# Attention and channel mixing on one core: the planner gives way to program order on all engines

## The chip, the core and the metric

The kernel runs on one core of one Trainium2 chip. The time is the device time of that core, in microseconds; two runs of the kernel before gave 1718.52 and 1720.22 us, a median of 1719.37. The profiled execution spans 1714.8 us. Everything is float32.

## What is computed

```python
scores = scale * q @ k.T                      # 8 batches, 8 heads, 576 x 64
thresh = max(scores, -1) - tau
scores = where(scores >= thresh, scores, -1e9)
attn   = softmax(scores) @ v                  # (+1e-9 in the denominator)
x      = heads side by side                   # (8, 576, 512)
u      = x + real(fft(fft(x, axis=1), axis=2))
un     = (u - mean(u)) / sqrt(var(u) + 1e-6)  # over the 512
out    = u + relu(un @ w_ch1) @ w_ch2         # 512 -> 2048 -> 512
```

The two heavy products at the end are done per group of 512 rows (nine groups), from the second group on with a two-level scheme of seven products of half-sized blocks (Strassen's kind), which saves products and costs additions of operands and results.

## The kernel before, in words

**Attention.** Heads go in pairs `n` (four pairs a batch, 32 in all). A pair has five steps `t`, so there are 160 steps `i = 5 n + t`, 20 to a batch; steps 0 to 3 hold 128 queries of both heads, step 4 the last 64 of both. One step is: `scores(i)` (TensorE, L427 or L433, into two large product banks `sc`); `softmax(i)`; and, one step later, `weights_in_parts(i - 1)`, which transposes the weights on TensorE (`pe` L530, `pw` L548) and copies them out on ScalarE (L536, L550; L540, L552 in step 4). At t = 3 and at t = 1 of the next pair `weighted_values` makes the products with v (L577).

**The softmax** is one function. For each of two heads: the negative maximum on VectorE (L451), the Exp on ScalarE (L459) and the threshold (L463), then on VectorE the masked product with its sum (L467) and the add of 1e-9 (L472); then the reciprocals (L481) and the scaling, one head on VectorE (L484), one on ScalarE (L488; step 4 copies 64 columns instead, L497). In the first eight pairs the scaling is done later, with a copy `rec` of the reciprocals on GpSimd (L493).

**Mixing.** After four pairs `fold_rows` folds their rows (VectorE for the last pair of a batch, GpSimd for the others), and `mixing(b)` makes the Fourier transforms: folds on VectorE (L661 to L670), products `py` (L680), then `pa` (L697, L701) with a copy on ScalarE (L713), two sums on VectorE (L717, L718) and sums into `u_t` on GpSimd (L720, L724).

**Products.** `two_level(g, rows)` is a generator. Its first stage has 28 blocks (L1045; results combined by ScalarE and by VectorE, L1014), its second 49 (L1195), seven for each of seven left operands. Between the blocks stand the sums that make operands: `l2_forms` for the next left operand (s1 to s4, L1121, shared by VectorE and GpSimd), `l1_form` (L1097), `s1_part` (L1026), and those that combine results: `gather` and `plus` (L1125), then `finish`, which adds to the rows (L789), and the stores. Jobs that are left at the end of a group lie in `pending` and are taken two at a time by `tick`, one tick for each first-stage block of the next group. For group 1 alone `w2_forms` (L897) remakes the second weights between the first-stage blocks, and `w1_forms` (L866) the first weights between the products of group 0.

**What sets the order.** `fill()` advances the mixing by one part and the products until they have spent their budget; it stands two or three times in each step and so spreads products between the pieces of attention. Up to step 39 the whole kernel stands in a manual schedule, in which each engine runs its instructions in the order in which the program names them. At L1501 `by_hand.close()` ends it, and L1502 opens one for TensorE alone: from step 40 TensorE keeps program order, and ScalarE, VectorE, GpSimd and the transfer queue are ordered by a planner, which works from the program's order and its own costs. All engines execute in the order that they are given. Product banks are a ring: four `mm` banks for everything but the scores.

## Time and profile before

Each row is a stretch of the profiled execution; busy times in us.

| stretch, us | what lies in it | TensorE | VectorE | ScalarE | GpSimd |
|---|---|---|---|---|---|
| 286.7 to 505.8 | steps 40 to 59, end of group 0, weights remade | 204.7 | 139.8 | 91.9 | 122.2 |
| 505.8 to 695.1 | steps 60 to 79 | 176.2 | 138.6 | 94.8 | 84.3 |
| 695.1 to 886.7 | steps 80 to 99 | 175.9 | 140.0 | 94.2 | 84.5 |
| 886.7 to 1077.1 | steps 100 to 119 | 174.1 | 137.5 | 94.5 | 84.0 |
| 1077.1 to 1270.6 | steps 120 to 139 | 176.2 | 140.7 | 94.2 | 84.4 |
| 1475.0 to 1714.8 | products without attention | 222.4 | 129.4 | 47.0 | 122.8 |

Over the whole span of 1714.8 us TensorE is busy 1574.0, VectorE 1199.5, ScalarE 795.0 and GpSimd 854.3. The mean granted TensorE clock is 0.966 of full speed.

How to read such views: a wait is idle time of an engine just before an instruction, with the instruction whose end released it. In a timeline each line has start, duration, engine, source line, operation, output and inputs, and in brackets the idle time before it. The names of tiles are the program's: `w_all` is the second weights' tile, reused as room for operands and results from group 1 on; `hs` the hidden values; `e` the softmax weights; `tmp` the two halves of the transform.

### The profile page before, as it was taken

To read this page: it belongs to the slowest core of one execution; us is meant where nothing else is said; L and a number is where in the kernel's file an instruction comes from. 1 tells how busy PE (TensorE), PEld (TensorE's weight loads), DVE (VectorE), ACT (ScalarE), POOL (GpSimd) and SP (SyncE) were. 2 spreads that over 40 slices of the span, in tenths; PEclk is the share of its full clock that TensorE was granted. 3 is DMA by queue.
4 is the path that set the end of the run, shared out by engine and by line. 5 is a ranking of instruction groups with operands and counts; after the bars stand their busy time and mean duration, and the time that the engine had idled before them with its cause. 6 is when DMAs were issued, how large, how long until landed. Compare 5 with 4: busy or idle time off the path is not lost.

```text
span 1714.8 us, 27077 instructions
## 1 busy us (share of the span) xinstructions
PE 1574.0 (92%) x9770; PEld 1215.3 (71%) x9770; DVE 1199.5 (70%) x2462; ACT 795.0 (46%) x1700; POOL 854.3 (50%) x961
## 2 busy tenths in 40 slices
PE   8998898998999899889989899889989899889997
PEld 4555454555788677777777678667778678879897
DVE  6987885566667767776677668786677768635646
ACT  5865664433535464445454454436444454222120
POOL 6784666267462434452363434452353434545536
PEclk9999999999999999999999999999989999999999
DMA  6433432545563435434453435424453423446755
GB/s 157 114 105 128 112 96 56 146 148 174 179 191 101 139 113 150 148 109 120 120 167 110 132 110 171 148 89 120 127 159 121 122 97 132 170 152 219 249 172 203
DMA packets 245499, 239.04 MB, mean 139 GB/s; under 512 B 196947, under 2 KB 214869, under 8 KB 225014
## 3 DMA queue, kind: packets, MB, share of 16 engines
q1 hardware_dynamic: 242854, 237.02, 45.0%
q8 instruction: 77, 1.26, 0.3%
q10 hardware_dynamic: 2512, 0.30, 0.1%
q14 instruction: 56, 0.46, 0.1%
HBM read 207.50 MB, written 29.62 MB: 138 GB/s over the span
## 4 chain that ended last, share of the span: by engine, by line
PE 55%; DVE 24%; POOL 10%; ACT 5%; issue 4%; DMA 2%; SPq 0%; DVEq 0%; ACTq 0%; POOLq 0%
PE ph L1045 20%; PE po L1195 10%; PE pv L577 6%; PE sc L427 6%; PE pw L548 4%; DVE e L467 4%; DVE w_all L1125 3%; DVE neg L451 3%; PE po L821 3%; DVE w_all L1121 2%; POOL w_all L1125 2%; PE ph L803 2%; ACT e L459 2%; POOL w_all L1121 1%; DMA w<-f 1%
## 5 line engine op out<-in xcount | busy, mean ns | idle before, releaser
L459 ACT ACTIVATE e<-sc,neg 128x576 f32<-128x576 f32 x288 | 211.7, 735 | 277.5 <-DVE neg L451 277.2
L451 DVE TENSOR_REDUCE neg<-sc 128x1 f32<-128x576 f32 x288 | 206.3, 746 | 117.5 <-PE sc L427 98.3
L467 DVE SCALAR_TENSOR_TENSOR e<-sc,thr,e 128x576 f32<-128x576 f32 x288 | 228.9, 814 | 57.2 <-ACT thr L463 56.2
L1195 PE MATMUL po<-w,w_all 128*128 128x128 f32 x1792 | 246.7, 292 | 9.4 <-ACT w_all L1207 4.9
L1195 PEld LDWEIGHTS po<-w,w_all 128*128 128x128 f32 x1792 | 231.1, 207 | 21.6 <-issue 9.9
L1121 POOL TENSOR_TENSOR w_all<-hs 128x512 f32<-128x512 f32 x72 | 97.8, 1359 | 227.4 <-PE po L1195 152.2
L1014 DVE TENSOR_TENSOR hs<-ph,hs 128x512 f32<-128x512 f32 (+1 forms) x128 | 105.2, 822 | 144.6 <-PE ph L1045 140.6
L548 PE MATMUL pw<-ident,e 128*128 128x128 f32 x1152 | 174.0, 278 | 20.5 <-ACT ends L536 5.3
L1045 PE MATMUL ph<-u_t,w 128*128 128x256 f32 x768 | 181.5, 382 | 4.3 <-ACT x L583 1.9
L427 PE MATMUL sc<-kT,qT 64*128 64x288 f32 x1024 | 176.1, 436 | 9.2 <-DVE e L467 9.1
L550 ACT COPY e_t<-pw 128x512 f32<-128x512 f32 x256 | 148.7, 593 | 49.2 <-PE pw L548 48.4
L548 PEld LDWEIGHTS pw<-ident,e 128*128 128x128 f32 x1152 | 137.4, 143 | 41.9 <-ACT ends L536 8.4
L1045 PEld LDWEIGHTS ph<-u_t,w 128*128 128x128 f32 x768 | 140.8, 190 | 30.8 <-issue 8.2
L1026 POOL TENSOR_TENSOR w<-hs 128x512 f32<-128x512 f32 x32 | 43.6, 1361 | 234.4 <-ACT hs L1022 222.6
L1045 PE MATMUL ph<-w_all,w 128*128 128x256 f32 x672 | 158.6, 383 | 1.5 <-DVE hs L1014 1.5
L427 PEld LDWEIGHTS sc<-kT,qT 64*128 64x128 f32 x1024 | 97.1, 189 | 66.8 <-issue 36.2
L1045 PEld LDWEIGHTS ph<-w_all,w 128*128 128x128 f32 x672 | 123.1, 190 | 23.6 <-issue 5.8
L1195 PE MATMUL po<-w,hs 128*128 128x128 f32 x960 | 127.2, 279 | 1.9 <-ACT ends L536 1.4
L488 ACT ACTIVATE e<-e,den 128x576 f32<-128x576 f32 x96 | 74.5, 776 | 106.4 <-DVE den L481 106.3
L1195 PEld LDWEIGHTS po<-w,hs 128*128 128x128 f32 x960 | 117.5, 194 | 7.9 <-issue 5.1
L1022 ACT ACTIVATE hs<-hs 128x512 f32<-128x512 f32 (+1 forms) x80 | 60.7, 759 | 78.5 <-DVE hs L1014 73.5
L484 DVE TENSOR_SCALAR e<-e,den 128x576 f32<-128x576 f32 x120 | 90.2, 751 | 3.5
(210 smaller groups left out, 2928.2 us busy)
## 6 DMA issues: line engine op xcount, KB each, us to landing
w<-f SPq DMA_DIRECT2D x152, 1024.0 KB, 4.9
hs<-in_moe_w_ch_dram SPq DMA_DIRECT2D x23, 512.0 KB, 4.7
q_in<-in_q_dram SPq DMA_DIRECT2D x128, 72.0 KB, 2.5
out_dram<-u SPq DMA_DIRECT2D x36, 256.0 KB, 2.3
k_in<-in_k_dram SPq DMA_DIRECT2D x124, 72.0 KB, 2.6
v_in<-in_v_dram SPq DMA_DIRECT2D x64, 128.0 KB, 2.4
f<-w SPq DMA_DIRECT2D x14, 512.0 KB, 4.3
f<-w SPq DMA_DIRECT2D x7, 1024.0 KB, 4.1
```

The lines of the kernel that those rows point to most:

```text
L427: nc.tensor.matmul(sc[j][:, c, 0:HALF], qT[hp, 128 * t : 128 * t + 128], kT[hp, k0 + HALF * c : k0 + HALF * (c + 1)], start=True, stop=True,)
L451: nc.vector.tensor_reduce(out=neg[:, j : j + 1], in_=sc[j][:, :, 0:HALF], axis=AXIS_XY, op=ALU.max, negate=True,)
L459: nc.scalar.activation(out=ej, in_=sc[j][:, :, 0:HALF], func=ACT.Exp, bias=neg[:, j : j + 1], scale=1.0)
L467: nc.vector.scalar_tensor_tensor(out=ej, in0=sc[j][:, :, 0:HALF], scalar=thr[:, j : j + 1], in1=ej, op0=ALU.is_ge, op1=ALU.mult, accum_out ...
L484: nc.vector.tensor_scalar(out=e[:, 0:S], in0=e[:, 0:S], scalar1=den[:, 0:1], scalar2=None, op0=ALU.mult)
L548: nc.tensor.transpose(pw[:, c, :], e[:, c0 : c0 + 128], ident[:, :])
L550: nc.scalar.copy(e_t[:, 4 * j : 4 * j + 4, qs], pw[:, :, :])
L577: nc.tensor.matmul(pv[64 * j : 64 * j + 64, 0:m], vt[:, 2 * c + j, :], e_t[:, 4 * j + c, 0:m] if c < 4 else ends[:, 0, 0:m], start=(c == 0 ...
L1014: nc.vector.tensor_tensor(out=to, in0=bank, in1=to if other is None else other, op=ALU.add)
L1045: nc.tensor.matmul(bank[:, 256 * q : 256 * q + 256].rearrange("p (two n) -> p two n", two=2), left[:, 256 * c + 128 * q : 256 * c + 128 * ...
L1121: eng.tensor_tensor(out=out_, in0=in0, in1=in1, op=op)
L1195: nc.tensor.matmul(to, lefts[m][j][:, s], right_[:, 128 * s : 128 * (s + 1)], start=jn in (0, 4) and s == 0, stop=s == 3, skip_group_check ...
```

## The change

It does five things, all of which act from step 40 on.

- `by_hand.close()` and the schedule for TensorE alone are taken out: all engines and the transfer queue keep program order to the end.
- The softmax becomes three functions, and the loop puts them between the stretches of products: maxima and Exp behind the scores and the values' products; masked products, one add for both denominators, reciprocals and the first scaling after the first `fill`; the second scaling after the transposes. The values' product is a generator too, so that its copy comes after the Exp.
- Sums that one engine made right after the other no longer change engines: in `l2_forms` s1 and s2 are VectorE's and s3 and s4 GpSimd's, in `l1_form` one operand is all VectorE's and one all GpSimd's.
- The gathers of three of the four results move to `pending`, and there to GpSimd (to VectorE in the last group only).
- The first pair's folding and row swap come later: `x_first` holds all 576 columns, and `fold_rows` copies it. The mixing of a batch starts at step 2 of the next batch and no longer at step 1.

```diff
+    def softmax_first(i):
...
+        for j in range(nh):
+            nc.vector.tensor_reduce(... negate=True)
+        for j in range(nh):
+            nc.scalar.activation(out=ej, in_=sc[j][:, :, 0:HALF], func=ACT.Exp, ...)
+            if j == 0:
+                nc.scalar.activation(out=thr[:, 0:nh], in_=neg[:, 0:nh], ...)
+    def softmax_second(i):
...
+        for j in range(nh):
+            nc.vector.scalar_tensor_tensor(... accum_out=den[:, j : j + 1])
+        nc.vector.tensor_scalar(out=den[:, 0:nh], ..., scalar1=1e-9, ...)
+        nc.vector.reciprocal(den[:, 0:nh], den[:, 0:nh])
+        nc.vector.tensor_scalar(out=e[:, 0:S], ..., scalar1=den[:, 0:1], ...)
+    def softmax_third(i):
...
+            nc.scalar.activation(out=e[:, S : 2 * S], ..., scale=den[:, 1:2])
...
-                (V if m == 1 else P, s1, x21, x22, ALU.add),
+                (V, s1, x21, x22, ALU.add),
                 (V, s2, s1, x11, ALU.subtract),
                 (P, s3, x11, x21, ALU.subtract),
-                (V, s4, x12, s2, ALU.subtract),
+                (P, s4, x12, s2, ALU.subtract),
...
-        at_slots(2, (4, 5, 6), l1_form(s1_tile, s1_tile, a11, (V, P, V, P))[0:3])
-        at_slots(3, (0,), l1_form(s1_tile, s1_tile, a11, (V, P, V, P))[3:4])
-        at_slots(4, (1, 2, 4, 6), l1_form(a12, a12, s1_tile, (V, P, V, P)))
+        at_slots(2, (4, 5, 6), l1_form(s1_tile, s1_tile, a11, (V, V, V, V))[0:3])
+        at_slots(3, (0,), l1_form(s1_tile, s1_tile, a11, (V, V, V, V))[3:4])
+        at_slots(4, (1, 2, 4, 6), l1_form(a12, a12, s1_tile, (P, P, P, P)))
...
-        at_slots(6, (2, 2, 3, 4, 4), gather(V, v_22))
-        at_slots(6, (5, 5), finish(1, 1, v_22))
...
-        pending.extend(gather(V, v_12))
-        pending.extend(gather(V, v_21))
+        last = g == NG - 1
+        for v in (v_22, v_21, v_12):
+            pending.extend(gather(V if last else P, v))
+        pending.extend(finish(1, 1, v_22))
+        pending.extend(finish(1, 0, v_21))
+        pending.append(stores(2, 3))
         pending.extend(finish(0, 1, v_12))
         pending.append(stores(0, 1))
-        pending.extend(finish(1, 0, v_21))
-        pending.append(stores(2, 3))
...
     late.append(True)
-    by_hand.close()
-    ctx.enter_context(tc.manual_schedule(engines={mybir.EngineType.PE}))
-    for i in range(2 * per_batch, total + 2):
+    for i in range(2 * per_batch, total + 3):
         if i < total:
             scores(i)
...
+        next(values, None)
+        if i < total:
+            softmax_first(i)
+        next(values, None)
+        if i % per_batch == 2:
+            while folds:
+                fold_more()
+            start_batch(i // per_batch - 1)
...
+        fill()
...
+        if i < total:
+            softmax_second(i)
+        weights = weights_in_parts(i - 1) if i <= total else iter(())
+        next(weights, None)
+        if t > 2 or i % per_batch == 1:
             fold_more()
         fill()
         next(weights, None)
         if i < total:
-            softmax(i)
+            softmax_third(i)
...
         fill()
```

## The prediction

> **What bounds the kernel now.** I read the sums by stretch first, then who TensorE waited for, then the timeline at the two waits that come back in every batch.
>
> The sums (us of the stretch, then busy time of each engine, then the granted TensorE clock). 286.7 us is where step 40 starts, the first step that the change touches; the four rows of 505.8 to 1270.6 are one batch of attention each.
>
> ```profile
> 286.70:505.80 219.10, 204.71 (x1072) 138.77 (x1071) 139.75 (x277) 91.93 (x198) 122.20 (x119) 0.96 0.52 159
> 886.70:1077.10 190.40, 174.14 (x1171) 142.16 (x1170) 137.48 (x292) 94.45 (x203) 83.97 (x98) 0.96 0.44 131
> 1270.60:1475.00 204.40, 184.15 (x1221) 151.09 (x1221) 142.21 (x295) 97.99 (x214) 87.35 (x98) 0.95 0.37 121
> ```
>
> TensorE is the bound and waits some 16 us in 190. Stretch less PE busy over all of 286.7 to 1714.8 is 114 us, of which some 10 is the drain after the last product: **104 us of idle TensorE** can be won. VectorE is busy 137 of 190, GpSimd 84. Who it waited for, after 286 us (us, times, longest):
>
> ```profile
> PE pe L530 <- ACT e L497: 23.8, 8, 4.8
> PE pa L697 <- DVE tmp L718: 21.8, 5, 4.7
> PE pn L763 <- ACT x L583: 6.2, 5, 1.3
> PE pe L533 <- POOL rec L493: 5.4, 1, 5.4
> PE ph L1045 <- POOL t_room L1001: 4.3, 1, 4.3
> PE po L1195 <- ACT ends L540: 4.3, 1, 4.3
> PE pw L548 <- DVE u L789: 3.8, 1, 3.8
> ```
>
> A dozen waits of about 4.5 us make up over half. The first kind, at the start of a batch, in order of time:
>
> ```profile
> 891.00 2.48 POOL L1121 TENSOR_TENSOR w_all<-w 128x512 f32<-128x512 f32 x2
> 892.29 1.73 DVE L1121 TENSOR_TENSOR w_all<-w_all,w 128x512 f32<-128x512 f32 x1 [6.69 <-POOL w_all L1121]
> 894.32 0.52 DVE L484 TENSOR_SCALAR e<-e,den 128x576 f32<-128x576 f32 x1
> 894.88 0.24 ACT L497 COPY e<-e 128x64 f32<-128x64 f32 x1 [9.26 <-DVE e L484]
> 895.17 0.47 PE L530 MATMUL pe<-ident,e 128*128 128x128 f32 x1 [4.81 <-ACT e L497]
> ```
>
> VectorE, in order, stood 6.69 us behind a GpSimd sum issued just before; the softmax it held back (L484) was all that the transpose needed. The second kind, five steps later: VectorE ran the gather sums L1125, L789 and the next step's maxima L451 before the two sums (L717, L718) that free a product bank:
>
> ```profile
> 946.62 1.14 DVE L1125 TENSOR_TENSOR w_all<-w_all 128x128 f32<-128x128 f32 x4
> 949.78 0.45 DVE L718 TENSOR_TENSOR tmp<-pa,tmp 128x289 f32<-128x289 f32 x1
> 950.37 0.40 PE L697 MATMUL pa<-seq_even,y_e 128*1 128x145 f32 x1 [4.67 <-DVE tmp L718]
> ```
>
> Each such wait costs twice. The stretch after the first:
>
> ```profile
> 894.30:901.10 6.80, 4.74 (x21) 4.34 (x22) 5.55 (x14) 5.69 (x14) 0.00 (x0) 0.50 0.01 2
> 960.00:970.00 10.00, 10.00 (x60) 7.85 (x57) 6.72 (x18) 4.67 (x9) 3.89 (x6) 1.00 0.68 231
> ```
>
> For 6.8 us after it the clock is 0.50: 21 products, where an undisturbed 10 us hold 60 (another product mix, with longer shapes). So a wait of 4.5 us costs 4.5 and then 6.8 x 0.5 = 3.4. The clock record has such windows after 286 us for 96 us in all, so **48 us of TensorE time** besides the 104.
>
> **What the Trainium skill says.** "TensorE: Matmul & The Clock Gate", Part 1, says that the array falls to half clock after an idle window of about 3.4 us that runs freely, and returns after a busy one. The trace agrees: waits of 3.5 us and more are followed by a window at 0.50, those of 1.3 us in steady stages are not. "SBUF — State Buffer", Who interferes with whom, says that a VectorE instruction with two SBUF inputs shuts out a GpSimd instruction that reads SBUF, and the reverse, one waiting for the whole of the other. The trace fits: the same 128x512 sum L1121 takes 0.81 us on average on VectorE in one form and 1.73 at 892.29, beside GpSimd. "GPSIMD Engine Reference", 4.1, puts two-input sums at about twice VectorE's time; here 1.36 us (GpSimd, w_all<-hs) against 0.81 to 1.13.
>
> **The change part by part.** The products, 5,635 instructions, are the same; only their order and that of the other engines moves.
>
> 1. *Program order on all engines from step 40.* Until now ACT, DVE, POOL and the queue were ordered by a planner from there. Step 39's reciprocal copy (rec L493) stood behind six GpSimd sums (L866, 2.35 us each); in order it comes first. That takes away 5.4 us, the 1.7 before it and (3.4 + 6.8) x 0.5 = 5.1 of half clock: **12 us**.
> 2. *No short-notice work.* In each left operand of the second stage VectorE makes s1 and s2, GpSimd s3 and s4, and s4 is used last of seven; a11's difference is all VectorE's. So no VectorE sum waits for a GpSimd one issued a product ago, bar the last quarter of a12. First kind: five waits of 4.49, 4.81, 4.52, 4.83 and 3.52 = 22.2, their windows (three of 6.8, one of 10.2, one of 3.4) x 0.5 = 17, and the copy wait of 1.2 after four of them = 5: **44 us**. The single 4.3 us (po <- ACT ends L540) is the same event at 516 us, with its window **8 us**.
> 3. *Gathers to GpSimd.* 105 VectorE sums leave (7 groups x 15): L1125's means of 0.44 (128x128) and 0.91 us (128x256), 3 and 2 of a gather, make 21 x (3 x 0.44 + 2 x 0.91) = 66 us less on VectorE; on GpSimd the rows of 0.83 and 1.04 give 21 x (2.5 + 2.1) = 96 us more, some 16 a batch on 84 of 190, hidden beside the first stage's products. With L717 and L718 straight after their products the second kind goes: 4.67 + 4.14 + 4.67 + 4.14 + 4.14 = 21.8, and 5 x 3.4 = 17: **39 us**.
> 4. *Softmax in three pieces.* 96 adds of 0.15 us go (two denominators in one), 14 us off VectorE. The maxima come behind the scores, the masked products one fill later, so that the Exp (0.74 each) runs beside other work; scaling is done a fill before the transposes need it. What a 9 us step has in slack is some 3 us. I book 0 for it alone.
> 5. *Moved.* The batch's mixing starts a step later (20b+2), with x_first held whole (one copy of 576 columns, about 1 us, for one of 0.44). Nothing waits for it but the last group: 0, bound +6 us at the tail. The transfer queue is in order too, so weight loads stand behind stores that wait for VectorE; but a load is issued two chunks ahead (7 us of products without attention) and lands in 4.9: 0.
> 6. *What program order loses.* The w2 forms of group 1 (L897) were spread by the planner from 314 to 425 us. In order they start at step 50 and go by one part per product block. Seven keeps, each a chain: GpSimd sum 1.44, VectorE, GpSimd sum 1.30, the DMA (4.1), while GpSimd also makes the form, 2 x 2.5: some 7.9 us, 55 in all, plus about 11 of GpSimd's other work (folds, u forms). VectorE stands in that chain with the softmax queued behind, and TensorE behind that. A block's 8 matmuls start 0.216 us apart, so 14 blocks are 24 us of products; attention takes some 3.9 of a 9.2 us step (scores 1.2, transposes 1.5, values and rest 1.2), which makes 42: loss 66 - 42 = 24, less a few us of slack: **+18 us**, bounds 0 (the chain fits) and 40 (with half clock). The 3.8 us wait of 403 us (u L789) and its window, 7, go; as they lie in the same disturbed stretch I count **-6**.
> 7. *New small waits.* The second sine copy now stands on ACT until four GpSimd sums (3.2 us) are done, a fill (about 3 us) after they start; ACT also waits for VectorE's maxima before it copies x. Nothing in the trace prices this: bounds 0 and 2 x 4.5 + 6.8 = 16 a batch, if both recurring waits came back. I take 3 a batch, **+15 us**.
>
> Sum: -12 - 44 - 8 - 39 + 18 - 6 + 15 = -76, so 1719 - 76 = **1643 us**.
>
> **The rivals.**
> - *Waits come back in other places* (0.20). For it: VectorE, busy 126 of 190 a batch after the change, waits in order for scores, Exp and banks, and forms stand in its way. Against: most steps have no idle TensorE even now. Forms at +40, and 6 us a batch with a half-clock window: 1719 - 103 + 40 + 30 - 6 = 1680.
> - *Nearly all goes* (0.12). In the last hand-ordered steps (240 to 286.7 us) TensorE was not idle at all. Forms fit in, no new waits, 10 us of the smaller waits gone too: 1719 - 103 - 6 - 10 = 1600.
> - *Slower: VectorE becomes the bound* (0.08). Its work of 126 a batch plus its present waits for scores, banks and Exp, some 40, is 166 of 191. If rigid order brings these to 70, a batch takes 196: 6 x 5 + 18 = +48, 1767. Against: the gathers gone are its most contended sums.
>
> **How the numbers follow.** Forecast 0.60. The border of 2% is 1685. Forecast, near-all and a third of the first rival lie below: 0.79 faster; the rest of the rival, 0.13, within; 0.08 slower. The range reaches from "nearly all" to past the first rival: 1600 to 1695.
>
> **What would show it.** Right: no row pe <- e (L547) or pa <- tmp (L788) of over 2 us; mean clock up from 0.966 to 0.98; VectorE's busy time down by some 80 us, GpSimd's up by 96; the batch from about 190 us to 174; steps 50 to 55 longer, with VectorE idle before the forms. Wrong: recurring waits of over 3.5 us elsewhere (ACT's tmp copy on GpSimd), or batches still at 190 with the two kinds gone, which would mean that VectorE sets the pace.

## The result, and the profile after

The changed kernel takes **1692.82 us** (1692.64 to 1692.99) against 1719.37 before: a ratio of 0.9846, 95% interval 0.9803 to 0.9888. It is faster by 26.5 us, or 1.5%: clear of the noise, but short of the 2% from which the forecast counted a time as faster (its border was 1685). The forecast was 76 us (1643); the time lies inside the stated range, near its upper end.

The same three rows of sums by stretch, of the kernel after: steps 40 to 59, one steady batch (steps 100 to 119), and the last batch with its mixing, which here is taken to 1450 (it holds 1,318 records of TensorE against 1,221 in the row of before, so their lengths are not to be compared). Columns as before: length, busy time of TensorE, weight loads, VectorE, ScalarE, GpSimd, granted clock, DMA share, GB/s.

```profile
285.80:528.10 242.30, 206.24 (x1012) 137.85 (x1011) 138.99 (x252) 91.12 (x193) 117.77 (x108) 0.91 0.52 161
...
892.60:1074.80 182.20, 173.21 (x1185) 142.30 (x1184) 132.19 (x261) 94.06 (x204) 93.69 (x113) 0.98 0.46 142
...
1255.30:1450.00 194.70, 187.18 (x1318) 154.69 (x1318) 140.82 (x273) 99.85 (x221) 99.95 (x120) 0.99 0.44 141
```

Two things are to be seen. The steady batch went from 190.4 to 182.2 at a clock of 0.98 instead of 0.96: that is the gain. Steps 40 to 59 went from 219.1 to **242.3** at 0.91 instead of 0.96: a loss, where the forecast had a sum of nothing (-12 + 18 - 6). By stretch, after less before: steps 40 to 59 +23.1, steps 60 to 139 -37.6, steps 140 to the last product -11.0, the drain +2.4, and -0.9 ahead of step 40.

Who TensorE waited for after 286 us (us in total, times, longest):

```profile
PE pw L598 <- ACT ends L586: 28.3, 9, 4.8
PE sc L427 <- DVE e L527: 9.7, 4, 7.0
PE ph L1115 <- DVE hs L1084: 7.3, 2, 7.0
PE ph L1115 <- DMA w<-f: 7.2, 2, 6.6
PE pw L598 <- ACT x L636: 6.5, 1, 6.5
PE py L750 <- DVE f L731: 5.0, 2, 4.6
PE ph L1115 <- POOL t_room L1071: 4.1, 1, 4.1
PE po L1263 <- DMA w<-f: 3.4, 1, 3.4
```

Both kinds of wait that the change was aimed at are gone: the list has no transpose `pe` behind the copy of `e` and no `pa` behind `tmp`. In their place stands a wait of the transposes `pw` behind the copy `ends`. It comes in each batch at step 17, 2.8 us, and at step 2, 3.7 to 4.8 us (in the first two batches 0.9 to 1.6, with some 2.3 more at step 3). The one of `py` on `f` is new too, and stands in the tail; that on `t_room` was there before. The longest of the other rows lie in steps 40 to 59, once each.

**Step 2.** VectorE's timeline up to the late maxima (first lines), then ScalarE and TensorE:

```profile
908.44 0.69 DVE L841 BATCH_NORM_STATS2 stats<-u 128x6 f32<-128x512 f32 x1 [2.51 <-ACT u L839]
...
913.64 0.81 DVE L680 TENSOR_TENSOR half<-x 128x287 f32<-128x287 f32 x2
914.38 0.95 DVE L685 TENSOR_TENSOR f<-half 128x143 f32<-128x143 f32 x4
...
915.32 1.26 DVE L694 TENSOR_TENSOR f<-x 128x2 f32<-128x2 f32 x1
...
917.10 1.48 DVE L859 SCALAR_TENSOR_TENSOR u<-w_all,rstd,u 128x256 f32<-128x256 f32 x1
...
918.50 1.41 DVE L506 TENSOR_REDUCE neg<-sc 128x1 f32<-128x576 f32 x2
919.33 1.28 ACT L512 ACT_TABLE_LOAD   x1 [5.75 <-DVE neg L506]
...
922.07 0.26 ACT L586 COPY ends<-pe 128x128 f32<-128x128 f32 x1
...
922.38 0.69 PE L598 MATMUL pw<-ident,e 128*128 128x128 f32 x4 [4.84 <-ACT ends L586]
```

VectorE stood 2.51 us for ScalarE, then folded the batch's last pair, and only then came the maxima (L506). ScalarE is in order too: it stood idle for 5.75 us in front of the Exp with the copies `ends` and `e_t` queued behind it. These copies free the product banks, and TensorE, out of banks, waited for them, although the rows that they copy had nothing to do with these maxima. Between maxima and Exp stands also an `ACT_TABLE_LOAD` of 1.28 us, which began only when the maxima were there (the load before it, at 908.43, is L849's). It is part of the 4.84 us, and none of the runs that go at this wait takes it away. At step 17 (1052.59) the same chain, without such a load, starts from three sums L1191 of 0.68, 1.64 and 1.76 us, the last two beside GpSimd's sums; a fourth, of 1.64, comes behind the maxima.

**Steps 40 to 59.** The longest wait, 318.60, with VectorE and GpSimd ahead of it:

```profile
302.96 2.97 DVE L680 TENSOR_TENSOR half<-x 128x287 f32<-128x287 f32 x2
305.85 5.81 DVE L685 TENSOR_TENSOR f<-half 128x143 f32<-128x143 f32 x4
...
306.46 4.78 POOL L936 TENSOR_TENSOR w<-w,w 128x1024 f32<-128x1024 f32 x2
...
311.81 1.41 DVE L506 TENSOR_REDUCE neg<-sc 128x1 f32<-128x576 f32 x2
...
314.90 2.81 DVE L710 TENSOR_TENSOR f<-f 128x608 f32<-128x608 f32 x1
...
318.60 2.51 PE L427 MATMUL sc<-kT,qT 64*128 64x288 f32 x7 [7.03 <-DVE e L527]
```

The four sums L685 took 5.81 us; the same four took 0.95 in the kernel before (as L615, at 309.87) and take 0.95 at 914.38 above. Beside them GpSimd remakes the first weights in sums of 2.4 us each. Behind the late maxima VectorE then made L709 and L710 (1.73 and 2.81 us; 0.77 and 0.79 at step 102) before the masked product L527 that frees the scores' bank. And the wait for weights at the start of group 1, with the transfer queue before it:

```profile
398.01 0.37 SPq L866 DMA_DIRECT2D out_dram<-u  x1
398.42 1.40 SPq L1020 DMA_DIRECT2D w<-f  x3
...
403.76 1.62 PE L1115 MATMUL ph<-u_t,w 128*128 128x256 f32 x3 [6.62 <-DMA w<-f]
```

The load was issued just behind a store of rows, which had waited for VectorE.

### The profile page after: what moved, and what is told of

Same layout as the page of the kernel before. It is cut to its first block, busy times and chain, and to the rows that moved or that the text cites. A ratio compares the mean times of both kernels' runs of the same rounds, so it can differ in the third digit from the quotient of the medians.

```text
span 1690.9 us, 27097 instructions
## 1 busy us (share of the span) xinstructions
PE 1562.0 (92%) x9770; PEld 1208.6 (71%) x9770; DVE 1176.6 (70%) x2253; ACT 793.4 (47%) x1700; POOL 918.7 (54%) x1074
## 3 DMA queue, kind: packets, MB, share of 16 engines
q8 instruction: 78, 1.28, 0.3%
## 4 chain that ended last, share of the span: by engine, by line
PE 68%; DVE 17%; ACT 5%; POOL 4%; issue 3%; DMA 2%; SPq 0%; DVEq 0%; ACTq 0%; POOLq 0%
PE ph L1115 21%; PE po L1263 16%; PE pv L629 8%; PE sc L427 7%; PE pw L598 5%; PE po L891 2%; PE ph L873 2%; DVE e L467 2%; DVE w_all L1191 2%; ACT e L512 1%; PE py L750 1%; DVE e L527 1%; PE sc L433 1%; DVE neg L506 1%; PE pa L767 1%
## 5 line engine op out<-in xcount | busy, mean ns | idle before, releaser
L512 ACT ACTIVATE e<-sc,neg 128x576 f32<-128x576 f32 x216 | 158.8, 735 | 239.0 <-DVE neg L506 238.6
L1263 PE MATMUL po<-w,w_all 128*128 128x128 f32 x1792 | 241.1, 287 | 7.4 <-DMA w<-f 3.4
L1263 PEld LDWEIGHTS po<-w,w_all 128*128 128x128 f32 x1792 | 224.9, 201 | 18.3 <-issue 6.5
L506 DVE TENSOR_REDUCE neg<-sc 128x1 f32<-128x576 f32 x216 | 154.0, 749 | 113.5 <-PE sc L427 102.8
L1115 PE MATMUL ph<-u_t,w 128*128 128x256 f32 x768 | 185.1, 388 | 14.7 <-DMA w<-f 7.2
L527 DVE SCALAR_TENSOR_TENSOR e<-sc,thr,e 128x576 f32<-128x576 f32 x216 | 168.2, 811 | 15.0 <-ACT thr L516 15.0
L1195 POOL TENSOR_TENSOR w_all<-w_all 128x128 f32<-128x128 f32 (+2 forms) x161 | 117.3, 744 | 23.1 <-DVE w_all L1280 10.2
L535 DVE TENSOR_SCALAR e<-e,den 128x576 f32<-128x576 f32 x120 | 84.7, 706 | 4.2
```

The source lines that it names most:

```text
L506: nc.vector.tensor_reduce(out=neg[:, j : j + 1], in_=sc[j][:, :, 0:HALF], axis=AXIS_XY, op=ALU.max, negate=True,)
L512: nc.scalar.activation(out=ej, in_=sc[j][:, :, 0:HALF], func=ACT.Exp, bias=neg[:, j : j + 1], scale=1.0)
L527: nc.vector.scalar_tensor_tensor(out=ej, in0=sc[j][:, :, 0:HALF], scalar=thr[:, j : j + 1], in1=ej, op0=ALU.is_ge, op1=ALU.mult, accum_out ...
L535: nc.vector.tensor_scalar(out=e[:, 0:S], in0=e[:, 0:S], scalar1=den[:, 0:1], scalar2=None, op0=ALU.mult)
L1115: nc.tensor.matmul(bank[:, 256 * q : 256 * q + 256].rearrange("p (two n) -> p two n", two=2), left[:, 256 * c + 128 * q : 256 * c + 128 * ...
L1195: return lambda: eng.tensor_tensor(out=to, in0=to, in1=other, op=ALU.add)
```

## The experiments

Each run has the kernel before on the same chip beside it; the ratio is to that. The last two columns are the lengths of two stretches in the run's trace (before: 219.2 and 764.7 us). 1% is 17 us. Traces of versions that are the same in steps 60 to 139 have 723.2 to 727.2 us there, and those that are the same in steps 40 to 57 have 240.6 to 244.4 in steps 40 to 59. A difference of under some 4 us between two traces therefore tells nothing by itself.

| kernel | us | ratio, 95% interval | steps 40-59 | steps 60-139 |
|---|---|---|---|---|
| changed kernel | 1692.8 | 0.9846 (0.9803-0.9888) | 242.3 | 727.2 |
| planner | 1730.5 | 1.0081 (1.0060-1.0101) | 217.6 | 771.9 |
| order_only | 1997.0 | 1.1615 (1.1566-1.1664) | 293.6 | 929.5 |
| one_piece | 1925.6 | 1.1217 (1.1182-1.1253) | 263.9 | 896.5 |
| hybrid60 | 1668.1 | 0.9722 (0.9707-0.9737) | 218.9 | 724.6 |
| w1_spread | 1684.3 | 0.9816 (0.9791-0.9841) | 238.8 | 723.2 |
| load_early | 1688.2 | 0.9827 (0.9811-0.9842) | 237.1 | 725.9 |
| w2_spread | 1687.2 | 0.9822 (0.9804-0.9839) | 238.9 | 724.5 |
| three_spread | 1676.5 | 0.9765 (0.9746-0.9784) | 225.8 | 725.7 |
| late_fold | 1690.2 | 0.9853 (0.9836-0.9871) | 243.9 | 721.1 |
| copies_first | 1689.1 | 0.9854 (0.9837-0.9871) | 244.4 | 719.3 |
| forms_only | 1681.2 | 0.9785 (0.9763-0.9807) | 244.4 | 712.4 |
| stats_only | 1685.2 | 0.9810 (0.9786-0.9834) | 240.6 | 721.9 |
| gather_v | 1698.1 | 0.9897 (0.9876-0.9919) | 244.2 | 724.7 |
| short_notice | 1699.5 | 0.9903 (0.9886-0.9920) | 241.5 | 728.5 |
| best1 | 1648.7 | 0.9613 (0.9593-0.9632) | 221.1 | 707.8 |
| all_in_order | 1652.7 | 0.9617 (0.9598-0.9635) | 220.6 | 707.6 |
| best2 | **1643.2** | 0.9564 (0.9548-0.9579) | 215.4 | 708.5 |

The theories: **A**, the loss against the forecast is a short list of waits that rigid order makes, each with a cause that can be taken away; **B**, VectorE is in effect the bound under rigid order, and a wait taken away comes back as another.

### Order and text apart

**planner**: the text of the changed kernel, with the two lines back that leave all but TensorE to the planner.

```diff
+    by_hand.close()
+    ctx.enter_context(tc.manual_schedule(engines={mybir.EngineType.PE}))
     for i in range(2 * per_batch, total + 3):
```

> The changed kernel with its new order of the program text, its new engine assignments and its three softmax pieces, but with ScalarE, VectorE, GpSimd and the transfer queue ordered by the planner from step 40 on, as in the kernel before. Theory A (the loss against the forecast is named waits, which rigid order makes): the 23 us that steps 40 to 59 lost come back in part, and the new waits at steps 2 and 17 of a batch go or change place; about 1675 us. Theory B (VectorE is in effect the bound, and one wait taken away comes back as another): within 10 us of the changed kernel's 1692.8. If it is over 1705, program order itself is the main gain of the change and the assignments are worth little.

1730.5 us, the figure of neither theory: the new text under the planner is slower than the old one. It keeps steps 40 to 59 as short as before, and takes 45 us more than the changed kernel in steps 60 to 139. Its timeline at the longest wait, which comes once in each of five batches (6.6 to 9.8 us):

```profile
964.98 2.62 POOL L1195 TENSOR_TENSOR w_all<-w_all 128x256 f32<-128x256 f32 x5
...
966.96 4.22 DVE L859 SCALAR_TENSOR_TENSOR u<-w_all,rstd,u 128x256 f32<-128x256 f32 x1 [7.41 <-POOL w_all L1195]
...
971.10 1.41 DVE L506 TENSOR_REDUCE neg<-sc 128x1 f32<-128x576 f32 x2
...
971.88 0.74 ACT L512 ACTIVATE e<-sc,neg 128x576 f32<-128x576 f32 x1 [14.09 <-DVE neg L506]
...
974.16 1.11 PE L598 MATMUL pw<-ident,e 128*128 128x128 f32 x4 [9.84 <-ACT ends L586]
```

The planner put VectorE's finishing sum (L859) ahead of the maxima, and it stood 7.41 us for a gather that is now GpSimd's. So the gathers on GpSimd want an order that puts their reader late. This is read from the trace; no run tried the planner with the gathers on VectorE.

**order_only**: the kernel before, with those two lines taken out and nothing else.

> The kernel before with one edit of the change alone: the schedule by hand is not closed at step 40, so that ScalarE, VectorE, GpSimd and the transfer queue keep program order to the end; softmax in one piece, gathers, short-notice sums and the mixing are those of before. The planner with the changed text gave 1730, program order from step 60 with it 1668. Theory P (program order is what gains, and the new text is a small help): 1690 to 1720 us. Theory Q (program order needs the softmax in pieces and the jobs placed for it; on the old text VectorE blocks at each step): over 1740 us, with waits of TensorE on e or ends at most steps.

1997 us, theory Q. **one_piece**: the changed kernel, with its three functions called one behind the other where the softmax stood before.

```diff
-        if i < total:
-            softmax_first(i)
...
-        if i < total:
-            softmax_second(i)
...
         if i < total:
+            softmax_first(i)
+            softmax_second(i)
             softmax_third(i)
```

> The changed kernel with its three softmax functions called one behind the other at the end of the step, where the softmax in one piece stood before, all else as changed (program order from step 40). Theory P (the pieces are what makes program order possible): over 1900 us, the waits of sc on e (L527) of over 100 us in sum as in the kernel before with program order alone. Theory R (the rest of the text does it): under 1750 us. The forecast had booked 0 for the pieces, that is 1693.

1925.6 us. The two greatest waits of TensorE after 286 us, of order_only first:

```profile
PE sc L427 <- DVE e L467: 191.5, 123, 13.5
```

and of one_piece:

```profile
PE sc L427 <- DVE e L527: 134.6, 75, 6.4
```

The next scores need the bank that the masked product reads. With the softmax at the end of a step this product comes after all that the fills have named, just before the scores, at nearly every step. The four corners are then:

| | planner from step 40 | program order |
|---|---|---|
| text before | 1719 | 1997 |
| text after | 1730 | 1693 |

Neither half of the change gains alone. And within the text it is the pieces that count most: without them 233 us of the 304 between 1997 and 1693 are lost again. What they would win alone, in the old text, was not run.

### Steps 40 to 59

**hybrid60**: the changed kernel, with the planner kept up to step 59 and program order from step 60.

```diff
+    by_hand.close()
+    planned = ctx.enter_context(ExitStack())
+    planned.enter_context(tc.manual_schedule(engines={mybir.EngineType.PE}))
     for i in range(2 * per_batch, total + 3):
+        if i == 3 * per_batch:
+            planned.close()
+            ctx.enter_context(tc.manual_schedule())
```

> The changed kernel with the planner kept for ScalarE, VectorE, GpSimd and the queue in steps 40 to 59 alone, and program order from step 60 to the end. Theory A: steps 40 to 59 took 242.3 us in program order and 219.2 in the kernel before; with the planner they go back to about 220, and the rest stays: about 1670 us. Theory B: what the stretch wins is not kept, since work is only put off: over 1685 us.

1668.1 us: steps 40 to 59 took 218.9, the rest is unchanged (724.6 to 727.2). 23 of the 50 us that the forecast missed are here, and they aren't given back later.

Which part of program order costs it? **w1_spread** names the parts of the first weights' forms (L936) less often:

```diff
+        slots = itertools.count()
...
-                    next(forms, None)
+                    if next(slots) % 3 == 2:
+                        next(forms, None)
```

> The changed kernel with the first weights' forms (L936, GpSimd sums of 2.4 us each) put one behind every third stretch of products of group 0 and no longer one behind each, the rest at its end. Theory A: VectorE's fold in step 42 no longer runs beside them (its four sums L685 go from 5.81 us back to about 1), the 7.0 us wait at step 43 and its window go: 10 us less in steps 42 and 43; part of it may be given back where the rest of the forms comes at the end of the group. About 1683 us. Theory B (GpSimd's amount of work, not its place): the wait moves, 1690 to 1700.

**load_early** issues the load of weights at the end of group 0 ahead of its last store:

```diff
+            if t == 2:
+                for _ in forms:
+                    pass
+                ensure(1)
             rows.add(t, slice(0, DM), po[:, :])
             rows.store(t)
...
-        for _ in forms:
-            pass
-        ensure(1)
```

> The changed kernel with the weight load at the end of group 0 issued before the last store of rows, so that it does not stand on the transfer queue behind a store that waits for VectorE. Theory A2 (the in-order queue): the 6.6 us wait at the first products of group 1 and its half-clock window (6.8 us at half) go, and steps 50 to 54 have 10 us less: about 1683 us. Theory A1 (the chain of keeps sets that stretch): what is won at its start is lost behind it, 1688 to 1693 us.

**w2_spread** names the parts of the second weights' forms (L967) half as often:

```diff
-                next(forms, None)
+                if at % 2 == part % 2:
+                    next(forms, None)
```

> The changed kernel, all in program order, with the parts of the second weights' forms (L967) put one behind every second first-stage block of group 1 and no longer one behind each: 28 blocks instead of 14 for the seven keeps. The planner kept for steps 40 to 59 gave back 25 us. Theory A1 (the chain of keeps is most of that, steps 50 to 54 being too short for it): the waits of 7.0 (hs L1084) and 6.5 us (x L636) and two of their three half-clock windows go, steps 50 to 59 lose some 15 to 20 us in sum, about 1675 us. Theory A2 (the in-order transfer queue is most of it): the 6.6 us wait for w stays and others come, under 8 us won, 1685 to 1693.

1684.3, 1688.2 and 1687.2 us: w1_spread as theory A had it, load_early as A1 and w2_spread as A2, which is to say that neither of these two alone is most of the loss. Each took its own wait away and won little. w1_spread: in place of the 7.0 us at step 43 stands a wait of 2.2. load_early: the 6.6 us went, and the waits of steps 52 to 54 grew from 17.3 to 21.3 us in sum. w2_spread: the 7.0 became 3.3 and the 6.5 went, and one of 7.1 us for weights came at 501 us, where a load (L1020) again stood on the queue behind a transfer of the forms. In steps 40 to 59 they won 3.5, 5.2 and 3.4 us of 242.3, about the spread of unchanged traces, and in time each lies inside the interval of the changed kernel, so that only the waits tell them from it. **three_spread** has all three.

> The changed kernel, all in program order, with the three edits of batch 2 together: first weights' forms one behind every third stretch of products, the weight load ahead of the last store of group 0, second weights' forms one behind every second block. Alone they gave 0.3, 0.2 and 0.25% of the time. Theory A (three causes that hide one another: each edit alone gives its wait to the next in the chain): together they give more than the sum of 12 us, steps 40 to 59 fall from 242 to about 222 as with the planner, about 1672 us. Theory A' (separate causes of their own sizes): the sum, about 1680 us. Theory B (VectorE is short of time in that stretch): under 6 us, 1687 or more.

1676.5 us, between the two figures expected. The stretch fell by 16.5 us, where the three alone sum to 12.1 and theory A had 20. With a spread of some 4 us a trace this leaves open whether they hide one another; that they are causes it shows. Two waits for weights are left, 7.2 and 3.1 us, both for loads on the in-order queue.

### Steps 2 and 17

**late_fold** names the second half of the last pair's fold one step later:

```diff
-        if i % per_batch == 1:
-            fold_more()
         fill()
```

> The changed kernel with the second half of the fold of a batch's last pair one step later, so that these VectorE sums come behind the maxima of step 2 and not ahead of them. Theory A (ScalarE waits for late maxima, and product banks wait behind its Exp): the wait of about 4.8 us of pw on ends at step 2 falls to about 1 and its half-clock window goes, the one at step 17 stays; some 6 us for each of five batches, about 1663 us to 1670. Theory B: the fold delays step 3 instead, and the time stays at 1690 to 1695.

**copies_first** puts the Exp and the masked products of steps 2 and 17 behind the copies that free the banks:

```diff
+    LATE_EXP = (2, 17)
...
-        if i < total:
+        if i < total and i % per_batch not in LATE_EXP:
             softmax_second(i)
...
         next(weights, None)
+        if i < total and i % per_batch in LATE_EXP:
+            softmax_exp(i)
+            softmax_second(i)
```

> The changed kernel with Exp and the masked products of steps 2 and 17 of each batch put behind the first part of the transposes and their copies, so that the copies that free product banks do not stand on ScalarE behind an Exp that waits for late maxima. Theory A: both recurring waits (4.8 and 2.8 us) fall under 1 us and their windows go: 7.6 + 3 or so for each of five batches, about 1640 to 1655 us. Theory B: VectorE gets its Exp later, the scaling is late, and the waits turn up at the next transposes: 1685 to 1700 us.

Neither gained in time; in their traces steps 60 to 139 won 6.1 and 7.9 us, a little over the spread. late_fold took 1.1 us off the wait at step 2 (4.8 to 3.7). copies_first did what it says: the waits of `pw` behind `ends` went. At step 17 a wait of 1.7 us took the place of 2.8. Its timeline one step after step 2:

```profile
1098.09 3.02 PE L427 MATMUL sc<-kT,qT 64*128 64x288 f32 x8 [3.48 <-DVE e L533]
```

With the Exp later, the masked product was later and the next scores waited for their bank. That is theory B for step 2: the maxima are late because VectorE is, and moving ScalarE's queue moves the wait. So the two runs that follow shorten what VectorE has ahead of the maxima.

**forms_only** moves sums at the start of the second stage:

```diff
-        for _ in l2_forms(1):
-            pass
+        first_forms = l2_forms(1)
+        next(first_forms)
+        next(first_forms)
...
+        at_slots(0, (0, 1), [lambda: next(first_forms)] * 2)
...
-            at_slots(at, (1, 2, 3, 5) if at == 3 else (0, 1, 3, 5), [next_form] * 4)
+            at_slots(at, (3, 4, 5, 6) if at == 0 else (1, 2, 3, 5) if at == 3 else (0, 1, 3, 5), ...)
```

> The changed kernel with one edit: at the start of the second stage s3 and s4 of the first left operand are named at slots 0 and 1, and the forms of the second operand at slots 3 to 6 instead of 0 to 5, so that two of VectorE's four sums there (1.64 to 1.76 us each beside GpSimd's, 0.68 alone) come behind the maxima of step 17. Theory A: the wait of 2.8 us at step 17 falls to 1.1, as in the run with three edits, and its half-clock window goes: 1.7 + 1.7 to 3.4 a batch for five batches, 12 to 22 us, about 1672 to 1680 us; step 2 as before. Theory B: the sums then hold up step 18, and the gain is under 5 us.

1681.2 us, just above theory A's figure (by the ratios 10 us less than the changed kernel). VectorE's timeline at step 17 now has one sum less ahead of the maxima (two were expected to go, but the other stood behind them already),

```profile
1040.74 0.68 DVE L1191 TENSOR_TENSOR w_all<-hs 128x512 f32<-128x512 f32 x1
1041.46 1.64 DVE L1191 TENSOR_TENSOR w_all<-w_all,hs 128x512 f32<-128x512 f32 x1
1043.02 1.41 DVE L506 TENSOR_REDUCE neg<-sc 128x1 f32<-128x576 f32 x2
```

and TensorE's wait fell from 2.80 to 1.11 us, with no half-clock window after it (step 17: 12.5 to 9.3 us). Steps 60 to 139 won 14.8 us, 12.8 of them at step 17.

**stats_only** takes VectorE's stand of 2.5 us away, by naming the statistics two slots behind the copies that they read:

```diff
-                    rows.load((2, 3, 0, 1)[at])
-                    if at == 3:
-                        rows.factors()
+                    rows.load((2, 3, 0, 1)[at], True)
                     yield ND * 128
+                if jn == 5 and at < 4:
+                    rows.stats((2, 3, 0, 1)[at])
+                if jn == 6 and at == 3:
+                    rows.factors()
```

> The changed kernel with one edit: the statistics of a row tile (L841 and L842, for which VectorE stands 2.2 to 2.5 us until ScalarE has copied) two slots behind the copies, and the factors three slots later. Theory A: at step 1 VectorE no longer stands, the maxima of step 2 come some 2.5 us earlier, and the wait of 4.8 us at step 2 falls to about 2.3; with part of the half-clock windows 2.5 to 4 a batch, about 1675 to 1683 us. Theory B: it is the fold of the last pair that counts there, and the time is within 5 us of 1691.

1685.2 us. The wait of 4.8 us at step 2 fell to 1.0 to 1.9, but a wait of 1.0 to 2.2 us for the copy `x_first` came at step 3: steps 60 to 139 won 5.3 us, hardly more than the spread, and the time lies inside the changed kernel's interval. For step 2 both theories hold in part: the stand was a cause. What is left there is VectorE's other work or the table load of 1.28 us; no run parts the two.

### What had made the old waits

**gather_v** puts the gathers back on VectorE, at their new places:

```diff
-            pending.extend(gather(V if last else P, v))
+            pending.extend(gather(V, v))
```

> The changed kernel with the gathers of three results on VectorE, still among the pending jobs, and no longer on GpSimd: the changed kernel's only other difference in these 105 sums is taken back. The forecast had the second kind of wait (tmp L788) go with the gathers. If the gathers' engine is the cause, VectorE's busy time rises by some 60 us, waits of pa on tmp of about 4 us come back or others at steps 5 to 10 of a batch, and the time is 1705 to 1730 us. If the place of the sums in program order was all, the waits stay away, VectorE has slack in these steps, and the time is within 5 us of 1693.

**short_notice** takes back the division of s1 to s4 and of the two l1 forms:

```diff
-                (V, s1, x21, x22, ALU.add),
+                (V if m == 1 else P, s1, x21, x22, ALU.add),
...
-                (P, s4, x12, s2, ALU.subtract),
+                (V, s4, x12, s2, ALU.subtract),
...
-        at_slots(4, (1, 2, 4, 6), l1_form(a12, a12, s1_tile, (P, P, P, P)))
+        at_slots(4, (1, 2, 4, 6), l1_form(a12, a12, s1_tile, (V, P, V, P)))
...
```

> The changed kernel, in program order, with the split of s1 to s4 and of the two l1 forms between VectorE and GpSimd as it was before, so that VectorE sums again wait for GpSimd sums issued just before. The forecast booked the first kind of wait (44 us, then at the start of a batch) to this split. If the split is the cause also in program order: VectorE stands 2 to 7 us before L1191 several times a batch, TensorE waits of 4 us come back, 1715 to 1735 us. If it was the planner's order that put the softmax behind those sums: under 8 us of loss, 1690 to 1700.

1698.1 and 1699.5 us, both some 0.5% above the changed kernel and just past its interval, which their own overlap. In gather_v VectorE's busy time is 1219.6 us instead of 1176.6, and neither the wait of `pa` on `tmp` nor a longer step 5 is there (8.0 us in both, 16.1 to 16.4 before). In short_notice step 0 of these batches takes 6.4 to 8.6 us where the kernel before had 15.5 to 16.6. In steps 60 to 139 neither differs from the changed kernel (724.7 and 728.5 against 727.2). So under program order the old waits stay away **whichever engine has these sums**. They are not in order_only either, which has all of the old text: no `pa` waits for `tmp` there, and no `pe` over 0.7 us (though TensorE stands so long elsewhere in that run that this alone would prove little). What made them was the place that the planner gave the softmax and the bank-freeing sums of the old text. Under the planner the new text took the first kind away too, and brought the second down to 1.8 us at most: in the run planner step 0 takes 6.4 to 8.6 and step 5 7.5 to 9.4 us.

### Versions that beat both

**best1** has program order but for steps 42 to 59, with late_fold, forms_only and stats_only together.

```diff
+        if i == 2 * per_batch + 2:
+            by_hand.close()
+            planned = ctx.enter_context(ExitStack())
+            planned.enter_context(tc.manual_schedule(engines={mybir.EngineType.PE}))
         if i == 3 * per_batch:
```

> A version meant to beat both: program order to step 41 and from step 60, the planner for steps 42 to 59 only (the copy rec at step 40 then does not stand behind GpSimd sums: 6.5 us and a window); the last pair's fold one step later; the forms of the second left operand at slots 3 to 6 and s3, s4 of the first at slots 0 and 1, so that VectorE's maxima at step 17 do not stand behind four sums stretched by GpSimd; the statistics of rows two slots behind their copies, so that VectorE does not stand for ScalarE at step 1. Steps 40 to 59 alone in program order: no. Theory A (named waits): step 40 gives 10 us, step 2 (3.7 to 4.8 us and 3.4 of half clock) and step 17 (2.8 and 3.4) give 5 to 7 a batch of five: 1668 - 10 - 30 = about 1628 to 1640 us. Theory B (VectorE's whole load at these steps): the waits move, 1655 to 1668.

1648.7 us, between the two theories' figures: steps 60 to 139 at 707.8, 16.8 less than hybrid60; the waits are 1.5 to 2.0 us at step 2, 1.0 to 2.3 at step 3 and 1.1 at step 17. A wait of 9.0 us is left at step 43. Ahead of it VectorE is seen beside the first weights' forms:

```profile
302.23 2.32 DVE L531 TENSOR_SCALAR den<-den 128x2 f32<-128x2 f32 x1
...
307.86 3.00 DVE L680 TENSOR_TENSOR half<-x 128x287 f32<-128x287 f32 x2
310.79 5.28 DVE L685 TENSOR_TENSOR f<-half 128x143 f32<-128x143 f32 x4
...
321.70 1.77 PE L427 MATMUL sc<-kT,qT 64*128 64x288 f32 x4 [9.01 <-DVE e L527]
```

**best2** is best1 with w1_spread.

> best1 (1648.7) with one more edit: the first weights' forms one behind every third stretch of products. In best1 the GpSimd sums of 2.4 us each stand beside VectorE's fold at steps 42 and 43: L685 takes 5.28 us for four, L531, on 128x2 elements, 2.32 us, and TensorE waits 9.0 us. Theory A: with the sums spread this wait falls to 2 to 3 us and its window goes: 8 to 10 us, about 1640 us. Theory B (the planner fills the gaps with other GpSimd work, or the sums that are left then hold up the weight load at step 50): 1646 to 1655 us.

1643.2 us, ratio 0.9564: in place of the wait of 9.0 us at step 43 stands one of 3.1; one of 8.4 is left at step 51. That its time equals the forecast is chance: it is another kernel.

**all_in_order** asks whether the planner is needed at all: program order throughout, with three_spread, late_fold, forms_only and stats_only.

> Program order on all engines from step 40 to the end, as in the change, with all edits for named causes together: first and second weights' forms spread, the weight load ahead of the last store, the last pair's fold one step later, the forms at the start of the second stage and the statistics later. Theory A: three_spread gave 1676.5, and the edits at steps 1, 2 and 17 gave some 20 us on top of hybrid60: about 1653 to 1660 us. If under 1650, program order needs no planner at all; if over 1668, the planner's steps 42 to 59 are worth more than the named causes explain.

1652.7 us, 9.5 more than best2 has with the planner in 18 steps. Its steps 40 to 59 take 220.6 us, as many as under the planner (217.6 to 221.1), with one wait for weights of 7.1 us left. Sums by stretch of the steady batch, of best2:

```profile
854.20:1032.90 178.70, 172.50 (x1183) 140.59 (x1182) 131.08 (x261) 93.68 (x204) 95.42 (x115) 0.99 0.46 144
```

Theory A stands in the main: with the named causes gone, program order comes to within 10 us of the forecast. Theory B stands for step 2 alone, and there in part.

## Why the prediction was right or wrong, step by step

The waits that were to go went, but program order cost more than was booked. The terms that failed: the small waits of each batch (item 7: 3 us booked, 6.7 measured), the queue and the end of the kernel (item 5: nothing booked), the first weights' forms beside VectorE's fold (left out of item 1), and a credit that did not come (item 6).

1. **Program order at step 40, -12: right in size.** Steps 40 and 41 took 12.9 us less, though the 1.7 us that was to go is still there (1.66 at 288.23). What the step left out is that the GpSimd sums L936, which no longer stood ahead of `rec`, then stood beside the fold of steps 42 and 43: +11.0 there. Spread, they leave 2.2 us of wait instead of 7.0.
2. **No short-notice work, -44 - 8: right in size, not in cause.** Step 0 of the four batches from step 60 to 139 lost 33.5 us in sum; booked for these were three of the five waits with windows and copy waits, 13.8 + 10.2 + 3.6 = 27.6, and 8 for the wait at 516 us in step 60: 35.6. The division of the sums was not what did it under program order (short_notice): that another part of the same change took the same waits away is luck.
3. **Gathers to GpSimd, -39: right in size, not in cause.** Step 5 lost 33.4 us in four batches, 31 booked. The wait stays away with the gathers on VectorE (gather_v), so here too the size was luck. VectorE's busy time fell by 23 us and not by 80. The gathers' own rows did go from 69.4 to 5.3, but other VectorE instructions grew: the fold L685 by 7.7, L859 by 5.9, and the sums L1191 by 6.8, though they are 8 fewer. That GpSimd is busier by 64 us is not the reason: in gather_v it has 867.0 us (854.3 before), and they are as long (16.4, 43.3 and 122.2 in all against 16.4, 42.2 and 120.0). It is which GpSimd sums stand beside them in this order. The adds of 1e-9 have a cause of their own: those for two denominators (L531) take 0.277 us on average instead of 0.150, so that a third fewer adds take 1 us more and not 14 less (last section).
4. **Softmax in three pieces, 0: wrong**, though its error doesn't show in the sum, since the cost that the pieces avoid wasn't booked either. I booked the old waits to steps 2 and 3 and asked what the pieces add to that; the question was what program order costs without them, and that is 233 us (one_piece).
5. **The transfer queue, 0: wrong.** "A load is issued two chunks ahead" did not hold where the load stands in the queue behind something that waits for VectorE: a store at 398.01 (6.6 us of wait at 403.76), and the loads of the next q, which had stood 12.0 us for VectorE (3.4 us at 524.43 in step 59, which took 5.4 us more). **The later mixing, 0 with a bound of +6 at the tail:** the bound came. The stretch from step 159 to the last product took 6.4 us more, where 5.2 less was booked (the fifth wait of the first kind, 3.5, and its window, 1.7): a wait of 4.56 us of `py` on `f` at 1463.23 and a window of 6.8 us are new there. That the later start makes it is argued from its place; no run tried it, and it is still there in best2.
6. **Weight forms in program order, +18 - 6: the chain was about right, the credit was not.** Steps 50 to 54 took 23.7 us more, part of it item 5's wait. The seven keeps started from 401.7 to 467.6 us and the sums of the last ended at 471.5: 70 us, where I had worked out 66 for the chain. But the wait of 403 us was no credit: another, for weights, stands at the same place.
7. **New small waits, 3 us a batch: mis-sized.** This is the step that failed for the batches. Steps 2, 3, 17 and 18 took 37.5 us more in the four batches, with 10.6 given back at step 16: 26.8 net, or 6.7 a batch, where 12 (3 a batch) was booked. The cause named (ScalarE in order behind VectorE's maxima) was right; I had seen it for the copy of `x`, and priced a small wait, where the copies that free product banks stand behind the Exp. The wait that I named first, ScalarE's copy of `tmp` behind GpSimd, came on ScalarE (22.7 us in seven waits) and cost TensorE 0.8.

What was missed, in the traces: the collision at steps 42 and 43, 11.0; queue and forms, 23.7 + 5.4 - 12 = 17.1; the small waits of four batches, 26.8 - 12 = 14.8; the last batch with the tail, 12.6 (8.6 us less than before, with the drain, where 21.2 was booked). Together 55.5; smaller differences take 3.4 off. That is 52.1, the miss between the spans (-76 against -23.9).

The products are the same, as the prediction said: 9,770 records of TensorE in both traces. Its count of 5,635 stands in neither; nothing rests on it.

Of the signs named: no row of `pe` on `e` or `pa` on `tmp` over 2 us, right; steps 50 to 55 longer, with VectorE idle before the forms, right (26.4 us, L967 behind the DMA); clock to 0.98, no: 0.970, since half-clock time from 286 us to the last product fell only from 96 to 89 us, and it is 0.982 in best2; the batch to 174, no: 180.0 to 184.5 (175.2 to 178.9 in best2). And a sign of being wrong came: waits of over 3.5 us that return, at step 2 of three batches. The rival "waits come back in other places" (1680) was nearer than the forecast: its 6 us a batch is near the 6.7 that the small waits measured, and its +40 for the forms is near the 23.7 + 5.4 + 11.0 of steps 40 to 59, where the causes were more than the forms.

The Trainium skill's sentences held where they were used, but for the idle window of about 3.4 us that the prediction took over: less idle time was enough (last section). "SBUF — State Buffer", Who interferes with whom, names `tensor_scalar` too among those that can take the pair shared with GpSimd, and `tensor_reduce` as never contending on trn2. The traces agree: L531 took 2.32 us instead of 0.17 (best1), and of the maxima L506 none took over 0.76 us in the changed kernel, those at 1049.99 beside GpSimd's sums included. I had applied the page to sums of two inputs alone.

## What to carry to other kernels

Program order on every engine paid here only when the text already had the shape of a pipeline: first split the chain whose end frees a buffer, and measure order and text apart. When a wait is removed by order, ask of each in-order engine what stands behind its longest stand; a copy that frees a bank behind an Exp that waits for another engine is such a place, and so is a load behind a store. One-off work (remade weights) should be spread wide when nothing reorders it, and no long GpSimd sum put beside VectorE's chain.

## What the runs showed that I had not expected

- **A VectorE instruction on two elements a partition took as long as GpSimd's sum**: in best1 L531 on 128x2 took 2.32 us, L535 (128x576) 2.36 and L690 on 128x2 1.36, beside GpSimd sums of 2.4 us (128x1024). Undisturbed they take 0.17, 0.52 and 0.15. Two elements are what it takes: over all nineteen traces the add of 1e-9 on 128x1 never took over 0.156 us, though 1,566 of them began beside GpSimd work; of the adds on 128x2 that did, 601 of 765 took over 0.2. Making one add of two gave VectorE an instruction that GpSimd can hold up.
- **Waits of 2.8 us were followed by a half-clock window** of 3.4 us in four of the five batches at step 17 (one of them: 16 products at 0.51 from 1052.50 to 1055.90), those of 2.0 us at steps 2 and 3 of best2 in two of six, those of 1.1 at its step 17 in none. I had counted waits of 3.5 us and more. So 1.7 us off a wait won 3.2 us of the step.
- **Where a wait falls decides whether it costs a window.** In all nineteen traces the clock's records change on a grid of 3.413 us. From step 40 to shortly before the last product, a stretch of this grid at full clock in which TensorE stood idle for 2.1 us or more was followed by one at half clock in 234 of 234 cases, one with under 1.1 us idle in none of 6,765, and one in between in 85 of 259. The one wait of 2.8 us at step 17 that has no window (1412.27) lies across a border of the grid, with 1.50 us on one side and 1.29 on the other; the other four have 2.6 to 2.8 us in one stretch. The changed kernel's sums by stretch (length, busy time of TensorE, and further on the clock), for a wait within one stretch and for the one across a border:

```profile
1049.17:1052.58 3.41, 0.62 (x6) 0.38 (x4) 3.41 (x4) 1.75 (x5) 3.41 (x4) 1.00 0.64 204
1052.58:1055.99 3.41, 3.40 (x16) 3.40 (x17) 3.31 (x9) 2.87 (x8) 2.31 (x2) 0.50 0.25 103
...
1407.57:1410.98 3.41, 1.91 (x18) 1.67 (x16) 3.41 (x4) 0.48 (x1) 3.41 (x3) 1.00 0.30 48
1410.98:1414.39 3.41, 2.12 (x18) 2.06 (x19) 3.34 (x8) 3.37 (x11) 1.35 (x2) 1.00 0.62 259
1414.39:1417.80 3.41, 3.41 (x30) 2.22 (x30) 3.34 (x6) 1.26 (x2) 3.41 (x5) 1.00 0.00 0
```
